# Reordering the setup of an FFT convolution: tables while h loads, x behind four tables, spectrum of h and first x stage interleaved

**Chip, cores, metric.** One core of one Trainium2 chip. The metric is device time in microseconds (us) of one execution. Besides it, this study uses landmarks: start times of named instructions in one profiled execution, counted from the start of its span.

## What is computed

```python
# x: (8, 5696, 128), h: (5696, 128)
Xf = np.fft.rfft(x, n=2*S, axis=1); Hf = np.fft.rfft(h, n=2*S, axis=0)
y  = np.fft.irfft(Xf * Hf[None], n=2*S, axis=1)[:, :S]       # causal convolution per channel
theta = y @ w_theta
out   = u + relu(u @ w_ch),  u = y + w_tok_r @ (y*cos(theta)) + w_tok_i @ (y*sin(theta))
```

The convolution is a Fourier transform of length 11392 = 178 x 64 written as matrix products: stage a (89 points by table `f`, line 190), a product with table `w` (line 208), a product with the spectrum of h, stage c (tables `r_u`, `r_v`, line 320) and stage d (table `e`). It runs once over h and then in eight groups over x. The token-mixing products after it (line 910) run from 591 us to the end, nearly three quarters of the time.

## The kernel before, as far as it matters

Every table is made on the chip: GpSimd writes an index and scales it to turns, VectorE rounds (by adding and subtracting a large constant) and subtracts, ScalarE takes sine and cosine.

```python
def turns_of(pattern, base, lanes, m, per, quarter=None):
    ...                                                     # t, k: two rotating f32 buffers, [P, 11 * NB]
    nc.gpsimd.iota(k, pattern=pattern, base=base, ...)                              # L147
    nc.gpsimd.tensor_scalar(t, k, lanes, 1.0 / per, op0=mult, op1=mult)             # L149
    nc.vector.tensor_scalar(k, t, MAGIC, None, op0=add)                             # L152
    nc.vector.scalar_tensor_tensor(t, k, MAGIC, t, op0=subtract, op1=subtract)      # L153
    return t, k
def absolute(k, r):
    nc.vector.scalar_tensor_tensor(k, r, -1.0, r, op0=mult, op1=ALU.max)            # L160

for k0 in (0, 15, 30): w_table(k0)
nc.vector.tensor_copy(h16[:NB], u_t[...])              # L224: h, one copy
x16s = {0: load_x(0)}                                  # L127: 16 loads, f32 to f16, issued by GpSimd
steps, a_h = stage_a(h16, True)                        # True: evicted by ScalarE and VectorE in turn
woven(steps, [w_table(k0) for k0 in (45, 60, 75)])
for c in range(NCK): h_chunk(c)                        # spectrum of h, 12 chunks
a0, load0, b0 = front(0)                               # stage a of x, evicted by ScalarE alone
woven(a0, [r_table(0), r_table(1), s_table] + load0)
woven(b0, [e_table(n0) for n0 in (0, 11, 22)])         # product of x's spectrum with h's
```

The order in which instructions stand on each engine is made from this by a list scheduler at build time; each engine then runs its own list strictly in order.

## Time and profile before

| | kernel before |
|---|---|
| median of 3 runs | 2176.37 us (2172.37 to 2180.45) |
| first matmul on h / first spectrum matmul / first matmul on x / first stage-c matmul | 14.85 / 30.72 / 50.45 / 86.59 us |
| busy in 0 to 87 us: VectorE, ScalarE, GpSimd | 67.8, 58.8, 41.2 us |

The prediction below shows the lines of the timeline for these landmarks and reads them. GpSimd's groups in setup are, with the number of instructions, busy us, mean ns and idle time before them (groups of 0 to 87 us):

```profile
L149 POOL TENSOR_SCALAR turn<-whole,lane 90x979 f32<-90x979 f32 x3 | 7.7, 2556 | 0.3
L149 POOL TENSOR_SCALAR turn<-whole,lane 128x960 f32<-128x960 f32 x6 | 7.1, 1188 | 0.5
L147 POOL IOTA whole<- 128x960 f32 x6 | 6.0, 1012 | 14.2 <-ACT w_t L164 14.2
L147 POOL IOTA whole<- 90x979 f32 x3 | 5.5, 1820 | 7.6 <-DVE sgn L282 4.1 <-ACT e_t L164 3.5
```

### The profile page before, as it was taken

To read this page: it belongs to the slowest core of one execution; us is meant where nothing else is said; L and a number is where in the kernel's file an instruction comes from. 1 tells how busy PE (TensorE), PEld (TensorE's weight loads), DVE (VectorE), ACT (ScalarE), POOL (GpSimd) and SP (SyncE) were. 2 spreads that over 40 slices of the span, in tenths; PEclk is the share of its full clock that TensorE was granted. 3 is DMA by queue.
4 is the path that set the end of the run, shared out by engine and by line. 5 is a ranking of instruction groups with operands and counts; after the bars stand their busy time and mean duration, and the time that the engine had idled before them with its cause. 6 is when DMAs were issued, how large, how long until landed. Compare 5 with 4: busy or idle time off the path is not lost.

```text
span 2175.5 us, 41105 instructions
## 1 busy us (share of the span) xinstructions
PE 1998.2 (92%) x15545; PEld 1125.1 (52%) x15723; DVE 1619.4 (74%) x2920; ACT 670.6 (31%) x984; POOL 857.1 (39%) x1572
## 2 busy tenths in 40 slices
PE   4788898763899999999999999899999999999998
PEld 4787888652344444444444444344444444444444
DVE  7767767767778888888877667667777777776867
ACT  5877877574132333333210000001111111111111
POOL 5301010002344645445466544354545453535350
PEclk8788889987899999999999999999999999999999
DMA  7356463579988989899999869687878787879794
GB/s 146 89 125 163 128 162 118 172 185 275 236 156 175 182 169 168 167 179 176 176 169 162 138 115 291 106 133 137 148 132 152 132 151 130 152 131 153 126 158 91
DMA packets 409382, 340.38 MB, mean 156 GB/s; under 512 B 83303, under 2 KB 363751, under 8 KB 408071
## 3 DMA queue, kind: packets, MB, share of 16 engines
q0 software_dynamic: 221312, 143.00, 48.7%
q1 hardware_dynamic: 183552, 179.93, 28.5%
q10 hardware_dynamic: 4320, 14.81, 1.8%
q8 instruction: 123, 2.02, 0.4%
q14 instruction: 75, 0.61, 0.1%
HBM read 381.83 MB, written 97.93 MB: 221 GB/s over the span
## 4 chain that ended last, share of the span: by engine, by line
PE 65%; DMA 5%; DVE 4%; issue 2%; ACT 2%; POOL 1%; SPq 1%; DVEq 0%; ACTq 0%; POOLq 0%
PE m L910 59%; DMA b<-z_hbm 3%; PE m L878 2%; DMA z_hbm<-zz 2%; DVE c L917 1%; PE v L680 1%; PE utp L673 1%; PE m L914 1%; DVE wt L591 1%; PE m L833 1%; POOL wb L582 1%; PE m L831 1%; ACT mag L404 0%; ACT red L405 0%; PE theta_ps L382 0%
## 5 line engine op out<-in xcount | busy, mean ns | idle before, releaser
L582 POOL DMA_DIRECT2D wb<-in_moe_w_tok_i_dram x720 | 387.9, 547 | 679.3 <-DVE wt L591 602.6
L591 DVE STREAM_TRANSPOSE wt<-wb 128x384 f32<-128x384 f32 (+2 forms) x720 | 360.2, 524 | 117.1 <-PE m L910 71.2
L582 POOL DMA_DIRECT2D wb<-in_moe_w_tok_r_dram x720 | 386.6, 548 | 146.2 <-DVE wt L591 107.0
L910 PE MATMUL m<-b,wt 128*128 128x512 bf16 x1803 | 425.7, 381 | 7.1 <-DVE wt L591 2.4
L910 PEld LDWEIGHTS <-wt 128*128 128x128 bf16 x1848 | 181.3, 98 | 225.0 <-issue 5.7
L917 DVE TENSOR_TENSOR c<-c,m 128x512 f32<-128x512 f32 x420 | 271.0, 671 | 0.4 <-PE m L910 0.4
L675 ACT ACTIVATE uts<-utp 128x512 bf16<-128x512 bf16 (+1 forms) x90 | 53.2, 592 | 607.3 <-PE utp L673 607.3
L320 PE MATMUL ps<-r_u,u_t 128*128 128x128 f16 x1024 | 133.0, 228 | 14.9 <-DVE u_t L304 11.7
L321 PE MATMUL ps<-r_v,v_t 128*128 128x128 f16 x1024 | 131.7, 227 | 0.0
L670 ACT ACTIVATE ub<-c 128x512 bf16<-128x512 f32 (+1 forms) x90 | 56.3, 628 | 224.9 <-DVE c L846 139.7
L127 POOL DMA_DIRECT2D x<-in_x_dram x64 | 34.2, 541 | 201.3 <-PE ps L190 189.3
L320 PEld LDWEIGHTS <-u_t 128*128 128x128 f16 x1024 | 106.0, 103 | 13.6 <-DVE u_t L304 13.5
L321 PEld LDWEIGHTS <-v_t 128*128 128x128 f16 x1024 | 104.9, 103 | 5.2 <-issue 3.7
L304 DVE TENSOR_TENSOR u_t<-xs,hs 128x1024 f16<-128x1024 f16 x96 | 69.6, 725 | 41.9 <-ACT xs L302 31.5
L302 ACT ACTIVATE xs<-ps 128x1024 f16<-128x1024 f32 x96 | 95.3, 1017 | 17.6 <-DVE v_t L304 8.7
L878 PE MATMUL m<-b,wt 128*128 128x512 bf16 x344 | 79.3, 387 | 15.3 <-ACT red L405 14.5
L190 PE MATMUL ps<-f_t,x 89*128 89x180 f16 x512 | 84.5, 310 | 8.0 <-ACT xs L302 5.9
L208 PEld LDWEIGHTS <-w_t 64*128 64x128 f16 x3240 | 65.5, 106 | 38.1 <-issue 24.7
L580 POOL COPY wb<-b 128x2 bf16<-128x2 bf16 x4 | 0.5, 179 | 213.2 <-DMA z_hbm<-zz 213.2
L190 PEld LDWEIGHTS <-x 89*128 89x128 f16 x512 | 73.8, 237 | 10.1 <-issue 9.4
L384 ACT ACTIVATE red<-theta_ps,magic 128x512 f32<-128x512 f32 (+1 forms) x46 | 31.6, 687 | 140.8 <-PE theta_ps L382 107.4
L623 ACT ACTIVATE yb<-tpz 128x512 bf16<-128x512 bf16 (+1 forms) x46 | 27.4, 597 | 153.6 <-PE tpz L621 137.4
(2713 smaller groups left out, 3824.5 us busy)
## 6 DMA issues: line engine op xcount, KB each, us to landing
wb<-in_moe_w_tok_r_dram POOLq DMA_DIRECT2D x352, 96.0 KB, 4.5
wb<-in_moe_w_tok_i_dram POOLq DMA_DIRECT2D x352, 96.0 KB, 5.0
wb<-in_moe_w_tok_r_dram POOLq DMA_DIRECT2D x352, 80.0 KB, 4.2
wb<-in_moe_w_tok_i_dram POOLq DMA_DIRECT2D x352, 80.0 KB, 3.7
hs<-hf_hbm SPq DMA_DIRECT2D x192, 128.0 KB, 3.2
cp_hbm<-c SPq DMA_DIRECT2D x88, 256.0 KB, 2.3
c<-cp_hbm SPq DMA_DIRECT2D x88, 256.0 KB, 4.0
out_dram<-c SPq DMA_DIRECT2D x88, 256.0 KB, 4.2
```

Of the source, the lines that this page charges most:

```text
L190: nc.tensor.matmul(ps[:, i // 2, (i % 2) * 2 * K1:(i % 2 + 1) * 2 * K1], lhs(q + i), f1_t[:NB], start=True, stop=True)
L208: nc.tensor.matmul(ps[:, e, j * HD:(j + 1) * HD], w_t2[rows, c0 + j, N2 * (1 - ri):N2 * (3 - ri)], a_st["a"][rows, ri * K1 + c0 + j, :], s ...
L302: nc.scalar.activation(xs[:, :, :, :ck], ps, AF.Copy)
L304: nc.vector.tensor_tensor(uv[r][:, :, :, c0:c0 + ck], xs[:, :, :, :ck], hv[:, r:r + 1, :, :ck].to_broadcast([P, 2, HD, ck]), op=mult)
L320: nc.tensor.matmul(o, u_t[:, at:at + P], r_u, start=True, stop=False)
L321: nc.tensor.matmul(o, v_t[:, at:at + P], r_v, start=False, stop=True)
L582: nc.gpsimd.dma_start(wb[32 * i:32 * i + 32, :ng, :nj * 64], bass.AP(tensor=a.tensor, offset=a.offset + row0 * S + p * H + i * QR + j0 * 6 ...
L591: nc.vector.transpose(wt.rearrange("p j t r -> p (j t r)").bitcast(F32).rearrange("p (j g t) -> p g j t", j=TJ, g=4)[:, :ng, :nj], wb[:, : ...
L670: nc.scalar.activation(ub[:m].rearrange("p b d -> p (b d)"), c[:m], AF.Copy)
L878: nc.tensor.matmul(ms[n // 2 * 2 + h], a[n][:, j, :, r], bts[jj][n % 2 * 2 + h][:, r, :], start=(n % 2 == 0 and jj == 0 and r == 0), stop= ...
L910: nc.tensor.matmul(ms[q], a[q][:, j, :, r], bts[jj][q][:, r, :], start=(jj == 0 and r == 0), stop=(jj == NJ - 1 and r == 1 and q not in left))
L917: nc.vector.tensor_tensor(c, z, ms[q], op=op)
```

## The change

The intent is to use the 12 us in which h is on its way for tables, to let the loads of x begin when four tables are made, and to run the spectrum of h and the first stage of x side by side. To make room, work per table is moved: the index is written once and reused, the rounding add goes from VectorE to GpSimd, the absolute value becomes a bit mask. Tables get smaller (9 of 640 columns and 5 of up to 623 in place of 6 of 960 and 3 of 979). Its core, cuts marked by `...`:

```diff
-        nc.gpsimd.iota(k, pattern=pattern, base=base, ...)
-        nc.gpsimd.tensor_scalar(t, k, lanes, 1.0 / per, op0=mult, op1=mult)
+        nc.gpsimd.tensor_scalar(t, index_[:m], float(base), lanes[:m], op0=add, op1=mult)
...
-        nc.vector.tensor_scalar(k, t, MAGIC, None, op0=add)
+        rounded.append(nc.gpsimd.tensor_scalar(k, t, magic[:m], 1.0, op0=add, op1=mult).ins)
         nc.vector.scalar_tensor_tensor(t, k, MAGIC, t, op0=ALU.subtract, op1=ALU.subtract)
...
-        nc.vector.scalar_tensor_tensor(k, r, -1.0, r, op0=mult, op1=ALU.max)
+        nc.vector.tensor_scalar(k.bitcast(I32), r.bitcast(I32), 0x7FFFFFFF, None, op0=ALU.bitwise_and)
...
+    r_table(0, r_u); r_table(1, r_v); s_table()                      # moved up, before the w tables
-    for k0 in (0, 15, 30): w_table(k0)
-    nc.vector.tensor_copy(h16[:NB], u_t[...])
-    x16s = {0: load_x(0)}
+    for k0 in range(0, 4 * TW, TW): last[k0] = w_table(k0)           # TW = 10
+    for d0 in range(0, HD, 16):
+        with tc.issue_after(last[TW]):                               # behind the second w table
+            nc.vector.tensor_copy(h16[:, :, :, d0:d0 + 16], u_t[...])
...
+                with tc.issue_after(rounded[-1]) if bp == 0 else ExitStack():   # each x load of pair 0
...
+    woven(steps, x_steps[:2] + w_steps[:1] + x_steps[2:4] + w_steps[1:2] + x_steps[4:])
-    for c in range(NCK): h_chunk(c)
-    woven(a0, [r_table(0), r_table(1), s_table] + load0)
-    woven(b0, [e_table(n0) ...])
+    steps, a_st = stage_a(..., g == 0)                               # first x stage on ScalarE and VectorE
+    woven((h_chunks, 0.0, 0.9), (a0, 0.1, 1.0), (load0, 0.6, 1.0), (w_steps[2:], 0.0, 0.4), (e_steps[:2], 0.5, 1.0))
+    woven(b0, (e_steps[2:], 0.0, 0.8))
```

`issue_after` fixes a place in an engine's order; it does not wait for anything.

More of the change, by code (lines that the diff above doesn't have):

```diff
@@ L13 @@
 F16 = mybir.dt.float16
+I32 = mybir.dt.int32
 add = mybir.AluOpType.add
@@ L114 @@
     uv = [t[:, :UVW].rearrange("p (e d k) -> p e d k", e=2, k=K1) for t in (u_t, v_t)]
-    h16 = s1.tile([P, 2, N2, HD], F16)
     for p0, p1 in ((0, 80), (80, NB)):
@@ L119, with part @@
                                     ap=[[N2 * D, p1 - p0], [1, N2 * D]]))
+    x16s = {}
     def load_x(bp):
-        x16 = fx.tile([P, 2, N2, D], F16, tag="x16", name="x16")
-        for e in range(2):
+        def part(e, n0):
+            if (e, n0) == (0, 0):
+                x16s[bp] = fx.tile([P, 2, N2, D], F16, tag="x16", name="x16")
             src = x[2 * bp + e]
-            for n0 in range(0, N2, 16):
-                for p0, p1 in ((0, 80), (80, NB)):
+            for p0, p1 in ((0, 80), (80, NB)):
+                with tc.issue_after(rounded[-1]) if bp == 0 else ExitStack():
                     nc.gpsimd.dma_start(
-                        x16[p0:p1, e, n0:n0 + 16, :].rearrange("p n d -> p (n d)"),
+                        x16s[bp][p0:p1, e, n0:n0 + 16, :].rearrange("p n d -> p (n d)"),
                         bass.AP(tensor=src.tensor, offset=src.offset + (p0 * N2 + n0) * D,
                                 ap=[[N2 * D, p1 - p0], [1, 16 * D]]))
-        return x16
-    lane = fc.tile([P, 2], F32)
+        return [lambda e=e, n0=n0: part(e, n0) for e in range(2) for n0 in range(0, N2, 16)]
+    lane = fc.tile([P, 5], F32)
     for p0 in (0, 64):
@@ L138, with index @@
                    allow_small_or_imprecise_dtypes=True)
-    def turns_of(pattern, base, lanes, m, per, quarter=None):
+    for c, (src, per) in enumerate(((1, N1), (0, NF), (1, NF)), 2):
+        nc.vector.tensor_scalar(lane[:, c:c + 1], lane[:, src:src + 1], 1.0 / per, None, op0=mult)
+    TW, TE = 10, 7
+    def index(pattern, pool, tag="index"):
         n = 1
@@ L144, in turns_of @@
             n *= c
-        t = s2.tile([P, 11 * NB], F32, tag="turn", name="turn")[:m, :n]
-        k = s2.tile([P, 11 * NB], F32, tag="whole", name="whole")[:m, :n]
-        nc.gpsimd.iota(k, pattern=pattern, base=base, channel_multiplier=0,
-                       allow_small_or_imprecise_dtypes=True)
-        nc.gpsimd.tensor_scalar(t, k, lanes, 1.0 / per, op0=mult, op1=mult)
+        k = pool.tile([P, n], F32, tag=tag, name="index")
+        nc.gpsimd.iota(k, pattern=pattern, base=0, channel_multiplier=0, allow_small_or_imprecise_dtypes=True)
+        return k
+    rounded = []
+    def turns_of(index_, base, lanes, m, quarter=None):
+        n = index_.shape[1]
+        room, small = (P, "_s") if n <= P else (TW * N2, "")
+        t = s2.tile([P, room], F32, tag="turn" + small, name="turn")[:m, :n]
+        k = s2.tile([P, room], F32, tag="whole" + small, name="whole")[:m, :n]
+        nc.gpsimd.tensor_scalar(t, index_[:m], float(base), lanes[:m], op0=add, op1=mult)
         if quarter is not None:
             quarter(t)
-        nc.vector.tensor_scalar(k, t, MAGIC, None, op0=add)
+        rounded.append(nc.gpsimd.tensor_scalar(k, t, magic[:m], 1.0, op0=add, op1=mult).ins)
         nc.vector.scalar_tensor_tensor(t, k, MAGIC, t, op0=ALU.subtract, op1=ALU.subtract)
@@ L166, with r_table, quarter @@
     f1_t = fc.tile([P, 2 * K1], F16)
-    t, k = turns_of([[1, K1]], 0, lane[:NB, 1:2], NB, N1)
+    t, k = turns_of(index([[1, K1]], s1, "f_index"), 0, lane[:, 2:3], NB)
     sine(f1_t[:NB, K1:], t, -1)
     cosine(f1_t[:NB, :K1], t, k)
+    r_u = fc.tile([P, P], F16)
+    r_v = fc.tile([P, P], F16)
+    sgn = fc.tile([P, N2], F32)
+    def r_table(n_, r_):
+        def quarter(t):
+            nc.vector.tensor_scalar(t, t, 1.0 / N2, None, op0=mult)
+            for q0 in range(2):
+                for q1 in range(2):
+                    a_ = t[64 * q0:64 * q0 + 64, 64 * q1:64 * q1 + 64]
+                    nc.vector.tensor_scalar(a_, a_, 0.25 * (1 + n_ + q0 - q1), None, op0=add)
+        t, k = turns_of(r_index, 0, lane[:, 0:1], P, quarter)
+        sine(k, t, 1)
+        nc.vector.tensor_scalar(r_[:, :N2 + EN], k[:, :N2 + EN], 0.125, None, op0=mult)
+        nc.vector.tensor_scalar(r_[:, N2 + EN:], k[:, N2 + EN:], -0.125, None, op0=mult)
@@ new lines, in s_table @@
+    def s_table():
+        t, k = turns_of(s_index, 0, lane[:, 1:2], P, lambda t: nc.vector.tensor_scalar(t, t, 0.5, None, op0=mult))
+        absolute(k, t)
+        nc.vector.tensor_scalar(k, k, -4.0, 1.0, op0=mult, op1=add)
+        nc.vector.memset(sgn, 1.0)
+        nc.vector.tensor_scalar(sgn[:, EN:], sgn[:, EN:], k, None, op0=mult)
+    r_index, s_index = index([[0, 2], [1, N2]], s1, "r_index"), index([[0, 1]], s1, "s_index")
+    nc.vector.tensor_scalar(s_index, s_index, 1.0, None, op0=add)
@@ L171 @@
+    r_table(0, r_u)
+    r_table(1, r_v)
+    s_table()
     w_t2 = fc.tile([P, K1, 3 * N2], F16)
+    w_index = index([[1, TW], [N1, N2]], s1)
     def w_table(k0):
-        t, k = turns_of([[1, 15], [N1, N2]], k0, lane[:, 0:1], P, NF)
+        t, k = turns_of(w_index, k0, lane[:, 3:4], P)
         t3, k3 = (z.rearrange("p (k n) -> p k n", n=N2) for z in (t, k))
-        sine(w_t2[:, k0:k0 + 15, :N2], t3, 1)
-        cosine(w_t2[:, k0:k0 + 15, N2:2 * N2], t3, k3)
-        nc.vector.tensor_scalar(w_t2[:, k0:k0 + 15, 2 * N2:], w_t2[:, k0:k0 + 15, :N2],
-                                -1.0, None, op0=mult)
@@ L181, in stage_a @@
-    def stage_a(lhs, both=False):
+        sine(w_t2[:, k0:k0 + TW, :N2], t3, 1)
+        cosine(w_t2[:, k0:k0 + TW, N2:2 * N2], t3, k3)
+        return nc.vector.tensor_scalar(w_t2[:, k0:k0 + TW, 2 * N2:], w_t2[:, k0:k0 + TW, :N2],
+                                       -1.0, None, op0=mult).ins
+    def stage_a(lhs, both=False, home=None):
         st = {}
@@ L186, in chunk @@
             if q == 0:
-                st["a"] = fa.tile([P, 2 * K1, HD], F16, tag="a", name="a_")
+                st["a"] = (home or fa).tile([P, 2 * K1, HD], F16, tag="a", name="a_")
             ps = psum()
@@ L220, in woven @@
             f()
-    for k0 in (0, 15, 30):
-        w_table(k0)
-    nc.vector.tensor_copy(h16[:NB], u_t[:NB, :N2 * D].rearrange("p (n h d) -> p h n d", h=2, d=HD))
-    x16s = {0: load_x(0)}
-    steps, a_h = stage_a(lambda q: h16[:NB].rearrange("p h n d -> p (h n) d")[:, :, q], True)
-    woven(steps, [lambda k0=k0: w_table(k0) for k0 in range(45, K1, 15)])
+    last = {}
+    for k0 in range(0, 4 * TW, TW):
+        last[k0] = w_table(k0)
+    h16 = fa.tile([P, 2 * K1, HD], F16, tag="a", name="h16").rearrange("p k d -> p (k d)")[:NB, :N2 * D].rearrange(
+        "p (h n d) -> p h n d", h=2, d=HD)
+    for d0 in range(0, HD, 16):
+        with tc.issue_after(last[TW]):
+            nc.vector.tensor_copy(h16[:, :, :, d0:d0 + 16], u_t[:NB, :N2 * D].rearrange(
+                "p (n h d) -> p h n d", h=2, d=HD)[:, :, :, d0:d0 + 16])
+    steps, a_h = stage_a(lambda q: h16.rearrange("p h n d -> p (h n) d")[:, :, q], True, s1)
+    w_steps = [lambda k0=k0: w_table(k0) for k0 in range(4 * TW, K1, TW)]
+    x_steps = load_x(0)
+    woven(steps, x_steps[:2] + w_steps[:1] + x_steps[2:4] + w_steps[1:2] + x_steps[4:])
     hst = [t[:, :6 * D * CK].rearrange("p (c h d k) -> p c h d k", c=6, h=2, k=CK) for t in (u_t, v_t)]
-    nc.gpsimd.memset(hst[(NCK - 1) // 6][:, (NCK - 1) % 6], 0.0)
+    with tc.issue_after(rounded[-1]):
+        nc.gpsimd.memset(hst[(NCK - 1) // 6][:, (NCK - 1) % 6], 0.0)
     def h_chunk(c):
@@ L247, in h_chunk @@
                 h_[64 * ri:64 * ri + 64].rearrange("p h d k -> p h (d k)"))
-    for c in range(NCK):
-        h_chunk(c)
-    nc.gpsimd.memset(u_t[:, UVW:], 0.0)
-    nc.gpsimd.memset(v_t[:, UVW:], 0.0)
-    r_u = fc.tile([P, P], F16)
-    r_v = fc.tile([P, P], F16)
-    e_t = fc.tile([P, EN, 2, NB], F16)
-    sgn = fc.tile([P, N2], F32)
-    def r_table(n_, r_):
-        def quarter(t):
-            for q0 in range(2):
-                for q1 in range(2):
-                    a_ = t[64 * q0:64 * q0 + 64, 64 * q1:64 * q1 + 64]
-                    nc.vector.tensor_scalar(a_, a_, 0.25 * (1 + n_ + q0 - q1), None, op0=add)
-        t, k = turns_of([[0, 2], [1, N2]], 0, lane[:, 0:1], P, N2, quarter)
-        sine(k, t, 1)
-        nc.vector.tensor_scalar(r_[:, :N2 + EN], k[:, :N2 + EN], 0.125, None, op0=mult)
-        nc.vector.tensor_scalar(r_[:, N2 + EN:], k[:, N2 + EN:], -0.125, None, op0=mult)
+    e_t = fc.tile([P, EN, 2, NB], F16)
     def e_table(n0):
-        t, k = turns_of([[1, 11], [N2, NB]], n0, lane[:K1, 1:2], K1, NF)
+        n = min(TE, EN - n0)
+        t, k = turns_of(e_index[:, :n * NB], n0, lane[:, 4:5], K1)
         t3, k3 = (z.rearrange("p (n m) -> p n m", m=NB) for z in (t, k))
-        sine(e_t[:K1, n0:n0 + 11, 1, :], t3, -1)
-        cosine(e_t[:K1, n0:n0 + 11, 0, :], t3, k3)
-    def s_table():
-        t, k = turns_of([[0, 1]], 1, lane[:, 1:2], P, 2)
-        absolute(k, t)
-        nc.vector.tensor_scalar(k, k, -4.0, 1.0, op0=mult, op1=add)
-        nc.vector.memset(sgn, 1.0)
-        nc.vector.tensor_scalar(sgn[:, EN:], sgn[:, EN:], k, None, op0=mult)
+        sine(e_t[:K1, n0:n0 + n, 1, :], t3, -1)
+        cosine(e_t[:K1, n0:n0 + n, 0, :], t3, k3)
     LEAD = 4
@@ L361, in front @@
         x16 = x16s[bp].rearrange("p b n d -> p (b n) d")
-        steps, a_st = stage_a(lambda q: x16[:NB, :, dh * HD + q])
+        steps, a_st = stage_a(lambda q: x16[:NB, :, dh * HD + q], g == 0)
         return (steps, *stage_b(a_st, dh))
     a0, load0, b0 = front(0)
-    woven(a0, [lambda: r_table(0, r_u), lambda: r_table(1, r_v), s_table] + load0)
-    woven(b0, [lambda n0=n0: e_table(n0) for n0 in range(0, EN, 11)])
+    with tc.issue_after(rounded[-1]):
+        nc.gpsimd.memset(u_t[:, UVW:], 0.0)
+        nc.gpsimd.memset(v_t[:, UVW:], 0.0)
+        e_index = index([[1, TE], [N2, NB]], s1, "e_index")
+    e_steps = [lambda n0=n0: e_table(n0) for n0 in range(0, EN, TE)]
+    woven(([lambda c=c: h_chunk(c) for c in range(NCK)], 0.0, 0.9), (a0, 0.1, 1.0), (load0, 0.6, 1.0), (w_steps[2:], 0.0, 0.4),
+          (e_steps[:2], 0.5, 1.0))
+    woven(b0, (e_steps[2:], 0.0, 0.8))
     setup.close()
@@ L505, in next_x @@
             def next_x(bp=bp):
-                x16s[bp + 1] = load_x(bp + 1)
+                for part in load_x(bp + 1):
+                    part()
             a_ = a_ + [next_x]
```

## The prediction

> **What bounds the kernel now.** I read the page first, to see how much of the span the change can touch at all, then the timeline of the first 90 us, then the waits of that stretch, then the busy times by stage.
>
> The page, parts 2 and 4:
>
> ```profile
> PE   4788898763899999999999999899999999999998
> ...
> PE 65%; DMA 5%; DVE 4%; issue 2%; ACT 2%; POOL 1%; SPq 1%; DVEq 0%; ACTq 0%; POOLq 0%
> PE m L910 59%; DMA b<-z_hbm 3%; PE m L878 2%; DMA z_hbm<-zz 2%; DVE c L917 1%; PE v L680 1%; PE utp L673 1%; PE m L914 1%; DVE wt L591 1%; PE m L833 1%; POOL wb L582 1%; PE m L831 1%; ACT mag L404 0%; ACT red L405 0%; PE theta_ps L382 0%
> ```
>
> The end is set by TensorE: 59% of the chain is the token-mixing product (line 910), which the change does not touch. One slice is 54.4 us, and the first has TensorE at 4 tenths. Everything the change edits runs before the first matmul of stage c (line 320). The two programs' instruction orders were compared with line numbers and buffer numbers removed: beyond that point they are the same but for a few neighbours near the first stage c (and a swap of two neighbours late on TensorE). So the change is worth what it moves that one matmul, which the timeline puts at 86.59 us. Its landmarks:
>
> ```profile
> 12.51 2.29 DVE L224 COPY h<-u_t 89x8192 f16<-89x8192 f16 x1 [6.69 <-DMA u_t<-in_h_dram]
> ...
> 14.85 5.64 PE L190 MATMUL ps<-f_t,h 89*128 89x180 f16 x36 [14.85 <-DVE h L224]
> ...
> 20.11 0.99 POOL L147 IOTA whole<- 128x960 f32 x1 [9.47 <-ACT w_t L164]
> ...
> 30.72 4.42 PE L208 MATMUL ps<-a__163,w_t 64*128 64x64 f16 x159 [3.69 <-DVE a__163 L195]
> ...
> 50.45 0.92 PE L190 MATMUL ps<-f_t,x 89*128 89x180 f16 x4
> ...
> 63.61 3.35 PE L208 MATMUL ps<-a__707,w_t 64*128 64x64 f16 x128 [1.88 <-ACT a__707 L197]
> ...
> 86.59 0.29 PE L320 MATMUL ps<-r_u,u_t 128*128 128x128 f16 x1 [3.05 <-DVE u_t L304]
> ```
>
> Setup therefore has five legs: wait for h (to 14.85), first stage of h (to 30.7), spectrum of h (to 50.4), first stage of x (to 63.6), product with the spectrum (to 86.6). VectorE ends the last one. Busy time in three stretches (0 to 38, 38 to 63.6, 63.6 to 86.6):
>
> ```profile
> core 0: us, PE busy (x) PEld busy (x) DVE busy (x) ACT busy (x) POOL busy (x), PEclk, DMA share, GB/s
> 0.00:38.00 38.00, 15.38 (x244) 14.16 (x244) 24.16 (x35) 16.85 (x21) 23.78 (x42) 1.00 0.71 130
> 38.00:63.60 25.60, 15.82 (x244) 14.74 (x245) 21.21 (x37) 21.47 (x27) 12.50 (x12) 0.52 0.57 144
> 63.60:86.60 23.00, 12.38 (x373) 10.93 (x373) 21.98 (x32) 20.12 (x21) 4.95 (x2) 0.57 0.36 107
> ```
>
> From 38 us on VectorE is busy 43.2 of 48.6 us and ScalarE 41.6: these two share the bound. VectorE's large hole is early, 13.8 us before 38, nearly all of it while h loads. What filled its time, from the costliest groups of 0 to 87 us:
>
> ```profile
> L195 DVE CAST a__163<-ps 128x720 f16<-128x720 f32 x8 | 7.1, 898 | 0.0
> L160 DVE SCALAR_TENSOR_TENSOR whole<-turn 128x960 f32<-128x960 f32 x6 | 7.0, 1161 | 0.0
> L153 DVE SCALAR_TENSOR_TENSOR turn<-whole,turn 128x960 f32<-128x960 f32 x6 | 6.9, 1149 | 0.1
> ...
> L152 DVE TENSOR_SCALAR whole<-turn 128x960 f32<-128x960 f32 x6 | 3.9, 658 | 0.0
> ```
>
> **What the Trainium skill says.** "VectorE: DVE Perf Modes", section Mode 2×_2P: a one-source fp32 operation in SBUF uses both read ports and makes two results a cycle, an operation with two tensors cannot. The trace agrees: 658 ns against 1161 ns for the same 128x960. The new absolute value is a one-source operation, so I count it at the first rate; no record here shows a bitwise operation. "GPSIMD Engine Reference", section Specifications: GpSimd's SBUF interfaces are shared with VectorE, with contention when VectorE is in a two-port mode or has two SBUF inputs. The trace agrees: the 90x979 scaling on GpSimd took 1.40 us at 61.4 and 3.85 us at 67.5, beside products on VectorE. "DMA: Bandwidth & Descriptors", section SWDGE vs HWDGE vs iDMA: a cast during a transfer is to be had on the GpSimd path only. So the x loads (f32 to f16) must stand in GpSimd's program, and do: 12 of the 16 stood behind the iota that waited 9.47 us. "TensorE: Matmul & The Clock Gate", section What's actually happening: low activity halves the clock. Here it is 0.52 from 38 to 63.6 us; TensorE is busy 15.8 of 25.6 us there, so I give it no term.
>
> **The change part by part.** Sizes between measured ones are interpolated from 128 and 960 columns (tensor_scalar 0.23 and 0.66 us, two-input form 0.29 and 1.15, sine 0.40 and 1.10, GpSimd scaling 0.37 and 1.06): at 640 columns 0.49, 0.82, 0.83, 0.80 us.
>
> 1. Tables. The rounding add leaves VectorE (6 x 0.66 + 3 x 0.66 and small ones, about 6.4 us by their uncontended times) for GpSimd, which loses its 6 + 3 large iotas (11.5 us). Absolute values fall from 6 x 1.16 + 3 x 1.17 = 10.5 to 14 x 0.48 = 6.7 us. Smaller tables (9 of 640 and 5 of up to 623 in place of 6 and 3) add the fixed part of the other operations, some 2 us.
> 2. The first x stage is split between ScalarE and VectorE: 8 casts of 0.90 = 7.2 us come to VectorE, 8 of 0.83 leave ScalarE. Sum for VectorE: -6.4 - 3.8 + 2 + 7.2 = about -1. Its total of 67.4 us hardly falls; the gain has to come from filling the hole.
> 3. Start. Tables f, r_u, r_v, s and the first w run while h loads. h had landed at 12.5 with x traffic beside it; now some 12. The copy of 2.29 us becomes four of about 0.6, the first ending near 13.6: the first h matmul is about 1 us earlier.
> 4. First stage of h. VectorE between first copy and end: three copies 1.8, eight casts 7.2, w work 3.5 = 12.5 us, so it ends near 26 and the spectrum starts near 26.5, not 30.7: -4.
> 5. x. GpSimd's list up to the fourth table sums to about 10 us after 4.7, so the first x load issues near 15, not 5. The 16 loads are 8 x 320 + 8 x 36 KB = 2.9 MB; from 22 to 30 us x moved at 123 to 148 GB/s, mean 134: 21.8 us. Last landing about 37.5. In the kernel before, 0.7 MB had landed by 15 and the rest ran from 22 to about 38, yet its first x matmul was at 50.45, so x was not waited for. In the new TensorE order the first x matmuls stand after only two of twelve spectrum chunks: near 28.5 us the in-order engines reach x and stand until about 37.5. I expect a new wait of 7 to 9 us here; it eats step 4.
> 6. From there VectorE's order holds: 8 casts 7.2, 4.25 spectrum evictions 5.3, 8 absolute values 3.8, 3 negations 0.9, 7 subtractions 5.5, one scaling 0.45 = 23.1; then 22 products starting 0.605 apart and two short ones, 14.0. Sum 37.1, from 37.5 + 0.8 for the first four matmuls. Stalls: as before, 48.6 - 43.2 = 5.4 us. 38.3 + 37.1 + 5.4 = 80.8 us for the first stage-c matmul. ScalarE from the same point: 6.4 + 5.1 + 10.2 + 13.9 = 35.6, below VectorE.
>
> Gain: 86.6 - 80.8 = 5.8 us; 2176.4 - 5.8 = 2170.6. The change was presumably kept by its author for a gain, so I shade to 2170.
>
> **Rivals.** (a) x arrives early or its wait costs nothing, and the interleaved phase starts at 28.5: then VectorE ends at 28.5 + 0.8 + 37.1 + 5.4 = 72 us, a gain of 15 and 2162. Against it: the same 2.9 MB at the measured rate, issued later. (b) GpSimd becomes the bound: 8 tables x 2 operations x 0.8 us = 13 us after the last x issue near 29, but 2.4 to 3.9 us each where contended as at 57 and 67 us, which would pass 60 us and hold the last e tables, now all ahead of the first product in VectorE's order. That costs 3 to 8 us: 2173 to 2178. For it: doubled GpSimd arithmetic, more two-port work. Against: before, two thirds of such scalings were near 1.1 us. (c) The gain is swallowed later: nothing after is on a fixed clock, and the chain is TensorE work in order, so I take it as passed on whole.
>
> **Range and chances.** Setup is 87 us; 2% is 43.5, half of it. Neither rival comes near. The range takes rival (a) with a little more at its low end, 2161, and rival (b) at its high end, 2177; the three runs of before alone span 8 us. Faster by over 2%: 0.01; within: 0.98; slower: 0.01.
>
> **What would show it.** First h matmul near 13.6; first spectrum matmul near 26.5; a wait of TensorE for an x load of 7 us or more, ending at 36 to 39; first stage-c matmul near 81; absolute value of 640 columns near 0.5 us; the rest of the timeline shifted by one amount. Wrong if x comes before 32, if GpSimd holds VectorE before the products, or if the shift at stage c is not found at the end.

## The result

| | kernel before | changed kernel |
|---|---|---|
| median | 2177.46 us (4 runs) | 2178.61 us (4 runs) |
| range | 2172.37 to 2180.45 | 2174.57 to 2179.82 |
| ratio | | 1.0004, 95% interval 0.9981 to 1.0028 |
| first stage-c matmul | 86.59 | 85.89 us |

Nothing was gained. A ratio here and below is the mean time of one kernel's fast runs over that of the other's of the same rounds, so not quite the ratio of the medians. The forecast time, 2170, lay outside what was measured.

The landmarks in the timeline of the changed kernel (start and duration in us, engine, line, operation; in brackets how long the engine had stood and what ended that):

```profile
18.41 0.68 DVE L274 COPY h<-u_t 89x2048 f16<-89x2048 f16 x1
...
19.14 3.24 PE L235 MATMUL ps<-f_t,h 89*128 89x180 f16 x20 [19.14 <-DVE h L274]
...
32.23 1.89 PE L253 MATMUL ps<-a__205,w_t 64*128 64x64 f16 x64 [2.15 <-DVE a__205 L240]
...
38.59 1.47 PE L235 MATMUL ps<-f_t,x 89*128 89x180 f16 x8 [4.47 <-DMA x<-in_x_dram]
...
64.33 4.45 PE L253 MATMUL ps<-a__425,w_t 64*128 64x64 f16 x160 [1.33 <-DVE a__425 L240]
...
85.89 0.29 PE L347 MATMUL ps<-r_u,u_t 128*128 128x128 f16 x1 [2.44 <-DVE u_t L331]
```

Three readings. The copy of h has no wait in its brackets: h had landed, and the copy merely stood behind table work, so h starts 4.3 us later than before (19.14 against 14.85), not 1 us earlier. TensorE does stand for x, as predicted, but begins the spectrum only at 32.23 and so waits 4.5 us and not 9. And from x on the setup takes 47.3 us in place of the 43.3 predicted (37.5 to 80.8).

The busy times of the two stretches, before and after the first matmul on x:

```profile
core 0: us, PE busy (x) PEld busy (x) DVE busy (x) ACT busy (x) POOL busy (x), PEclk, DMA share, GB/s
0.00:38.59 38.59, 12.05 (x129) 11.24 (x129) 27.27 (x63) 19.15 (x26) 31.92 (x58) 1.00 0.64 120
38.59:85.90 47.31, 33.98 (x733) 29.01 (x733) 41.42 (x57) 38.75 (x44) 16.19 (x14) 0.85 0.52 139
```

In the first row the busiest engine is GpSimd: 31.9 of 38.6 us. In the kernel before it was busy 23.8 us of the first 38. GpSimd's groups of the changed kernel in 0 to 87 us:

```profile
L163 POOL TENSOR_SCALAR turn<-index,lane 128x640 f32<-128x640 f32 x9 | 9.7, 1081 | 6.8 <-DVE whole L174 6.4
L130 POOL DMA_DIRECT2D x<-in_x_dram x16 | 9.0, 569 | 0.5 <-DMA x<-in_x_dram 0.5
L166 POOL TENSOR_SCALAR whole<-turn,magic 128x640 f32<-128x640 f32 x9 | 9.0, 1000 | 0.2
L166 POOL TENSOR_SCALAR whole<-turn,magic 90x623 f32<-90x623 f32 x4 | 5.2, 1302 | 0.7 <-ACT e_t L178 0.4
L163 POOL TENSOR_SCALAR turn<-index,lane 90x623 f32<-90x623 f32 x4 | 4.3, 1086 | 9.1 <-ACT a__425 L242 6.8 <-DVE whole L174 2.3
```

The rounding add (line 166) takes 17.2 us here: 9.0 + 5.2 in these two rows, and 1.6 + 0.7 + 0.7 in the smaller groups. On VectorE it had been estimated at 6.4 us, and measured at 3.9 + 3.8 for the large tables. The iotas that were saved took 11.5. The sum of GpSimd in setup rose from 41.2 to 48.1 us. Its order shows what that does to x (GpSimd's timeline):

```profile
12.88 2.36 POOL L166 TENSOR_SCALAR whole<-turn,magic 128x128 f32<-128x128 f32 x3 [0.25 <-DVE turn L195]
15.77 1.31 POOL L163 TENSOR_SCALAR turn<-index,lane 128x640 f32<-128x640 f32 x1 [0.53 <-DVE whole L174]
17.17 0.89 POOL L166 TENSOR_SCALAR whole<-turn,magic 128x640 f32<-128x640 f32 x1
18.01 2.76 POOL L130 DMA_DIRECT2D x<-in_x_dram  x4
20.86 2.86 POOL L163 TENSOR_SCALAR turn<-index,lane 128x640 f32<-128x640 f32 x2
23.71 0.83 POOL L166 TENSOR_SCALAR whole<-turn,magic 128x640 f32<-128x640 f32 x1
24.49 2.11 POOL L130 DMA_DIRECT2D x<-in_x_dram  x4
26.64 0.81 POOL L166 TENSOR_SCALAR whole<-turn,magic 128x640 f32<-128x640 f32 x1
27.41 3.13 POOL L130 DMA_DIRECT2D x<-in_x_dram  x6
31.00 1.03 POOL L130 DMA_DIRECT2D x<-in_x_dram  x2 [0.47 <-DMA x<-in_x_dram]
```

GpSimd has hardly a gap from 13 to 32 us, and the x loads stand in between its table work: the first at 18.0, the last at 31.5 us. This list placed the x loads. From 23 to 27 us, after GpSimd had been at tables from 20.9 to 24.5, the transfers ran at 52 GB/s; from 27 to 32 us, with loads queued, they ran at 202 GB/s with the DMA engines busy throughout, so at the end of the list the transfers bind as well.

### The profile page after: what moved, and what is told of

The parts are those of the page before. It is cut to its first block, busy times and chain, and to the rows that moved or that the text cites. A ratio compares the mean times of both kernels' runs of the same rounds, so it can differ in the third digit from the quotient of the medians.

```text
span 2177.3 us, 41171 instructions
## 1 busy us (share of the span) xinstructions
PE 2001.1 (92%) x15545; PEld 1123.9 (52%) x15723; DVE 1621.2 (74%) x2938; ACT 669.3 (31%) x986; POOL 864.4 (40%) x1587
## 4 chain that ended last, share of the span: by engine, by line
PE 75%; DVE 8%; DMA 7%; ACT 4%; issue 3%; POOL 1%; SPq 1%; ACTq 0%; DVEq 0%; POOLq 0%
PE m L944 57%; PE m L912 3%; PE ps L347 3%; PE ps L348 3%; PE ps L235 2%; DMA b<-z_hbm 2%; DMA z_hbm<-zz 2%; DVE c L951 2%; PE ps L370 1%; DMA hs<-hf_hbm 1%; PE ps L253 1%; ACT xs L329 1%; PE v L714 1%; DVE wt L625 1%; PE utp L707 1%
## 5 line engine op out<-in xcount | busy, mean ns | idle before, releaser
L130 POOL DMA_DIRECT2D x<-in_x_dram x64 | 33.8, 535 | 204.2 <-PE ps L235 191.9
L329 ACT ACTIVATE xs<-ps 128x1024 f16<-128x1024 f32 x96 | 95.0, 1015 | 18.8 <-DVE v_t L331 9.8
L657 ACT ACTIVATE yb<-tpz 128x512 bf16<-128x512 bf16 (+1 forms) x46 | 27.5, 597 | 154.8 <-PE tpz L655 120.8
L417 ACT ACTIVATE red<-theta_ps,magic 128x512 f32<-128x512 f32 (+1 forms) x46 | 31.6, 687 | 136.1 <-PE theta_ps L415 107.3
```

The costliest lines, as they stand in the source:

```text
L329: nc.scalar.activation(xs[:, :, :, :ck], ps, AF.Copy)
```

## The experiments

The whole time tells apart 0.2% at best, about 4 us, so the first stage-c matmul is the main measure, and the whole time is given where it was taken in rounds. All runs but one were correct. Landmarks in us, busy times of VectorE (V), ScalarE (A) and GpSimd (G) before and after the first matmul on x:

| run | first h | spectrum | last x issue | first x | stage c | V, A, G to x | V, A, G from x | from stage c to the end |
|---|---|---|---|---|---|---|---|---|
| kernel before | 14.9 | 30.7 | 29.1 | 50.5 | 86.6 | 35.6, 25.6, 28.1 | 31.7, 32.9, 13.1 | 2088.9 |
| before_again | 15.0 | 30.8 | 29.3 | 50.5 | 86.6 | 35.6, 25.6, 27.8 | 31.7, 32.8, 13.3 | 2088.9 |
| changed kernel | 19.1 | 32.2 | 31.5 | 38.6 | 85.9 | 27.3, 19.2, 31.9 | 41.4, 38.8, 16.2 | 2091.4 |
| after_again | 19.2 | 32.2 | 31.2 | 38.7 | 84.8 | 27.0, 19.2, 32.3 | 41.6, 38.9, 16.2 | 2094.3 |
| h_early | 13.2 | 30.5 | 33.0 | 41.3 | 86.7 | 29.9, 19.3, 32.8 | 39.9, 38.7, 14.6 | 2091.3 |
| x_free | 16.0 | 32.6 | 32.5 | 40.7 | 86.3 | 29.4, 19.1, 35.7 | 40.1, 38.7, 14.8 | 2092.7 |
| hx | 13.6 | 32.0 | 32.5 | 39.5 | 85.0 | 30.3, 18.8, 33.0 | 40.0, 38.5, 14.8 | 2088.4 |
| pool_tiny | 16.2 | 27.2 | 26.7 | 33.8 | 76.4 | 28.9, 19.7, 25.6 | 38.0, 37.3, 6.5 | 2095.1 |
| round_dve | 19.2 | 32.3 | 27.2 | 34.4 | 81.7 | 29.2, 17.3, 22.8 | 45.3, 40.5, 9.4 | 2093.4 |
| a0_act | 19.1 | 32.2 | 31.4 | 38.6 | 86.9 | 27.2, 19.1, 32.1 | 35.5, 42.7, 14.2 | 2090.0 |
| seq | 19.1 | 32.2 | 31.5 | 50.0 | 83.0 | 36.9, 27.9, 39.4 | 29.0, 29.1, 10.5 | 2089.1 |
| seq_round | 19.2 | 32.2 | 27.0 | 48.1 | 82.2 | 42.7, 27.5, 26.6 | 31.7, 29.4, 5.6 | 2089.6 |
| seq_round_h | 13.3 | 31.6 | 32.3 | 49.2 | 83.3 | 41.7, 27.6, 26.7 | 31.8, 29.4, 5.6 | 2092.1 |
| seq_act_h | 13.7 | 29.1 | 32.4 | 50.3 | 83.2 | 35.3, 37.8, 26.5 | 29.0, 31.0, 2.8 | 2090.7 |
| act_only | 16.3 | 29.6 | 28.4 | 35.4 | 80.0 | 26.6, 25.6, 23.8 | 39.0, 43.1, 10.3 | 2091.5 |
| act_only_5 | 16.3 | 29.6 | 29.2 | 35.7 | 80.3 | 27.5, 25.6, 24.0 | 38.9, 43.1, 10.1 | 2091.6 |
| abs_old | 22.7 | 37.5 | 32.3 | 39.7 | 89.2 | 30.3, 18.0, 31.3 | 46.4, 41.1, 18.0 | 2090.6 |

One reservation holds for all of them. The list scheduler makes the orders anew for every edit, so no edited run changes one thing alone: of these runs only after_again has the changed kernel's order on VectorE. The first copy of h, for example, is the 40th of VectorE's instructions in the changed kernel, the 38th in act_only and the 44th in abs_old. No run holds the order fixed.

**Does a landmark repeat?** after_again is the changed kernel unaltered (no edit).

> The changed kernel unaltered, to learn how far its landmarks repeat. Every theory expects the first matmul on h at 19 us, the first on x at 38 to 39 us and the first stage-c matmul at 85 to 87 us (85.9 before). If the last one moves by 2 us or more, differences of that size in the other runs mean nothing.

It came at 84.8 us: 1.1 us from the first look. The later before_again, the kernel before unaltered:

> The kernel before, unaltered. Every theory that compares landmarks needs the first spectrum matmul at 30 to 31.5 us, the first on x at 49.5 to 51.5 and stage c at 85.5 to 87.5. If stage c is below 84 or above 89, one look at each kernel is not enough to compare them.

It came at 86.6, as the first look. So differences of 2 us at stage c can be read, and the setup of the changed kernel ends 0.7 to 1.8 us before the old one. From stage c to the end, looks at one kernel differ by up to 3 us. The clock that TensorE was granted plays no part that shows: from 38 to 63.6 us it was 0.52 in one look at the kernel before and 1.00 in the other, with TensorE busy 15.8 us in both and the same landmarks to 0.1 us. So the low clock there, which the prediction puts down to low activity, did not come with the same activity a second time.

**Theories A and B.** A: the arrival of x ends the first half and VectorE's list the second. B: the gain was lost with the late copy of h. h_early:

```diff
+    r_table(0, r_u); last[0] = w_table(0)
-        with tc.issue_after(last[TW]):        # the copies
+        with tc.issue_after(last[0]):
+    with tc.issue_after(copied):              # VectorE's part of r_v, s, w(10), w(20), w(30) behind the copies
+        r_table(1, r_v); s_table(); ...
```

> The four copies of h are queued behind table w(0) alone, and the tables r_v, s, w(10), w(20), w(30) behind the copies. Theory A (what ends setup is the arrival of x and the VectorE work queued behind it): the first matmul on h falls from 19.1 to 13.5 to 14.5 us, the first on x stays at 38 to 39 us, and the first stage-c matmul stays within 1.5 us of 85.9. Theory B (the gain was lost because h was copied 6 us after it had landed): the first stage-c matmul falls by 4 to 6 us, to about 81.

The copy came at 12.4 and the first matmul on h at 13.2, and stage c at 86.7: the 4 to 6 us of B do not appear. A holds for stage c but not for the way: x came 2.7 us later, and the spectrum began only 1.7 us earlier. TensorE's timeline shows where the 6 us went:

```profile
13.17 3.84 PE L233 MATMUL ps<-f_t,h 89*128 89x180 f16 x24 [13.17 <-DVE h L271]
22.07 1.46 PE L233 MATMUL ps<-f_t,h 89*128 89x180 f16 x8 [5.06 <-DVE a__205 L238]
```

After six chunks it stood 5.06 us for an eviction by VectorE, which stood in VectorE's order behind tables: VectorE worked on these from 15.4 to 21.1 us, with one gap of 0.3 us. Since x came later too, this run does not give the effect of an earlier h alone. Time over 4 runs: ratio 1.0011 (0.9994 to 1.0028). x_free:

```diff
-                with tc.issue_after(rounded[-1]) if bp == 0 else ExitStack():
+                with ExitStack():
```

> The x loads are no longer queued behind the fourth table; nothing else changes. First x issue about 11 us in place of 18.0, so x is complete near 32 in place of 38.4. Theory A: the first matmul on x falls to 33 to 34 us, and the first stage-c matmul by 3 to 5 us, to 81 to 83. Theory B: h is still copied at 18.4 or later, and the first stage-c matmul stays within 1.5 us of 85.9, because tables are held up by the issues on GpSimd.

The first x load was issued at 10.9 us in place of 18.0, and the last still at 32.5; x came 2 us later than in the changed kernel. A fails as well in what it said of this run: starting x early does not bring x early, since the loads are spread among GpSimd's table operations and move those back. Ratio 1.0008 (0.9985 to 1.0032). hx has both edits:

> Both edits together. Theory A alone: as x_free, 81 to 83 us for the first stage-c matmul. Theory B alone: as h_early, about 81. If each held the other (h first, then x), the two together give more than either: 76 to 79 us, and the whole kernel 2168 to 2172.

Stage c at 85.0, ratio 0.9999 (0.9976 to 1.0022): no gain either. With the changed kernel's, four orders of the same GpSimd work all end its last x issue at 31 to 33 us, with GpSimd busy for 79 to 88% of the time to x. That led to theory C.

**Theory C: GpSimd holds the setup.** pool_tiny takes GpSimd's large operations down to 16 columns and leaves every other engine its instructions (though not their order). Its output is wrong, which doesn't matter for the time.

```diff
-        nc.gpsimd.tensor_scalar(t, index_[:m], float(base), lanes[:m], ...)
+        nc.gpsimd.tensor_scalar(t[:, :16], index_[:m, :16], float(base), lanes[:m], ...)   # large tables only
-        rounded.append(nc.gpsimd.tensor_scalar(k, t, magic[:m], 1.0, ...).ins)
+        rounded.append(nc.gpsimd.tensor_scalar(k[:, :16], t[:, :16], magic[:m], 1.0, ...).ins)
```

> Wrong result on purpose: GpSimd's two operations per large table write 16 columns in place of 445 to 640 (the table buffers are filled once at the start, and the sines get a scale near zero so that their arguments stay legal); VectorE, ScalarE, TensorE and the transfers keep all their instructions. Theory C (GpSimd holds setup: its list delays the x issues, and its operations stretch VectorE's through the shared SBUF interface): last x issue falls from 31.5 to about 27, first matmul on x to 34 to 36 us, VectorE's busy time from there to stage c from 41.5 to 37 to 38.5 us, the first stage-c matmul to 77 to 81. Rival A (the work of VectorE and ScalarE sets it whatever GpSimd does): VectorE stays at 41 us busy or more and stage c at 84 to 86.

All four numbers moved as C said, two of them a little further: last x issue 26.7 (expected about 27), first x 33.75 (34 to 36), VectorE 37.96 us busy from there (37 to 38.5), stage c 76.4 (77 to 81), which is 9.5 us earlier than in the first look at the changed kernel. The stretch from x on:

```profile
33.75:76.40 42.65, 33.27 (x733) 28.82 (x733) 37.96 (x54) 37.30 (x43) 6.49 (x12) 0.87 0.57 152
```

Against the changed kernel's row above, 4.8 us of the 9.5 come before x and 4.7 after it. Two parts of C are not equally large. VectorE's busy time up to stage c is 66.8 in place of 68.7 us, with four buffer fills of 0.6 us more, so its other instructions took some 4.3 us less. VectorE's idle time fell from 17.2 to 9.6 us (85.9 - 68.7 and 76.4 - 66.8). Its waits that GpSimd ended up to stage c add up to 10.9 us in the changed kernel, 2.3 in pool_tiny and 7.7 in the kernel before; the wait for the rounded turns is the largest in the changed kernel (us in total, times, longest; then the same in pool_tiny):

```profile
DVE turn L167 <- POOL whole L166: 6.1, 7, 2.3
```

```profile
DVE turn L176 <- POOL whole L175: 1.1, 4, 0.4
```

So most of the gain is waiting for GpSimd's list that is gone.

round_dve undoes one line of the change, the place of the rounding add:

```diff
-        rounded.append(nc.gpsimd.tensor_scalar(k, t, magic[:m], 1.0, op0=add, op1=mult).ins)
+        nc.vector.tensor_scalar(k, t, MAGIC, None, op0=add)      # `rounded` takes the scaling operation instead
```

> The rounding add goes back from GpSimd to VectorE, all else as in the changed kernel. Theory C: GpSimd has 14 operations of about 1 us less, the last x issue comes near 26 and the first matmul on x at 33 to 36 us; VectorE gets 14 operations of 0.49 us more, 8 of them after that point, partly paid by shorter ones; first stage-c matmul 81 to 84. Rival A: VectorE only gains work, stage c at 87 to 90.

```profile
34.41 1.48 PE L235 MATMUL ps<-f_t,x 89*128 89x180 f16 x8 [0.17 <-issue]
...
81.74 0.29 PE L347 MATMUL ps<-r_u,u_t 128*128 128x128 f16 x1 [2.35 <-DVE u_t L331]
```

Last x issue 27.2 (expected near 26), first x 34.4 and no longer waited for, stage c 81.7: as C expected, although VectorE is busy 74.5 us in all in place of 68.7. The whole gain lies before x; from x to stage c it takes 47.3 us, as in the changed kernel. Rival A, which expected 87 to 90, fails. Ratio to the kernel before 0.9986 (0.9962 to 1.0009).

act_only gives the same line to ScalarE:

```diff
+        nc.scalar.activation(k, t, AF.Identity, bias=magic[:m])
```

> The changed kernel with the rounding add on ScalarE and the interleaving kept. Theory C: the first matmul on x again falls to 33.5 to 36 us, as with the rounding on VectorE, since GpSimd's list is the same; stage c at 80 to 84. If the place of the rounding mattered only through VectorE's load, the first matmul on x would stay at 38 to 39.

First x 35.4, stage c 80.0, the best of all correct versions. ScalarE paid 10.8 us (57.9 to 68.7 up to stage c). The sum of GpSimd up to there fell from 48.1 to 34.0. With more rounds:

> The changed kernel with the rounding add on ScalarE, again and timed. Stage c within 1.5 us of the 80.0 of the first look. If the 5 us at stage c are passed on to the end: ratio to the kernel before 0.996 to 0.9985. If something later swallows them: 0.9985 to 1.001.

Stage c again at 80.3, and 2174.00 us (5 runs) against 2177.41 for the kernel before (9 runs): ratio 0.9979, interval 0.9965 to 0.9992. The ratio lies where it was expected if the gain is passed on, though the interval reaches into the other range. This is the one version that is faster than the kernel before beyond the noise, by 0.2%; the changed kernel, at 1.0004, was timed in another round. Its timeline against that of the changed kernel:

```profile
35.74 1.47 PE L235 MATMUL ps<-f_t,x 89*128 89x180 f16 x8 [4.29 <-DMA x<-in_x_dram]
...
80.28 0.29 PE L347 MATMUL ps<-r_u,u_t 128*128 128x128 f16 x1 [2.00 <-DVE u_t L331]
```

**The other parts.** a0_act evicts the first x stage by ScalarE alone, as before:

```diff
-        steps, a_st = stage_a(lambda q: x16[:NB, :, dh * HD + q], g == 0)
+        steps, a_st = stage_a(lambda q: x16[:NB, :, dh * HD + q])
```

> The first x stage is evicted by ScalarE alone again: 8 casts of 0.90 us leave VectorE, 8 of 0.83 come to ScalarE, whose busy time after x goes from 38.8 to 45.5 of some 46 us. If VectorE alone ends setup, stage c falls by 3 us or more, to 81 to 83. If the two are balanced there, ScalarE takes its place and stage c comes at 86 to 90.

VectorE lost 6 us and ScalarE got 4; stage c at 86.9, 1 to 2 us later. That is in the second expectation's range, but hardly more than two looks at one kernel differ by: the first expectation, VectorE alone, fails, and the split of that stage was worth 2 us at most. abs_old puts the old absolute value back:

```diff
-        nc.vector.tensor_scalar(k.bitcast(I32), r.bitcast(I32), 0x7FFFFFFF, None, op0=ALU.bitwise_and)
+        nc.vector.scalar_tensor_tensor(k, r, -1.0, r, op0=mult, op1=ALU.max)
```

> The changed kernel with the absolute value in its old two-input form: 14 operations of 0.82 in place of 0.49 us on VectorE, 4.6 us in all, 2.5 of them after the first matmul on x. If VectorE's sum sets the end after x: stage c at 87 to 89.5. If GpSimd's list does, which the two-input form contends with as well: 85 to 87.

Stage c at 89.2, some 3 to 4 us later. This is not the bit mask alone: in the order made for this run the copies of h stand behind more table work, so the first matmul on h is 3.6 us later already (22.7 against 19.1). seq undoes the interleaving alone:

```diff
-    woven((h_chunks, 0.0, 0.9), (a0, 0.1, 1.0), (load0, 0.6, 1.0), (w_steps[2:], 0.0, 0.4), (e_steps[:2], 0.5, 1.0))
+    woven(h_chunks, (w_steps[2:], 0.0, 0.4))
+    woven(a0, load0, e_steps[:2])
```

> The interleaving alone is undone: twelve spectrum chunks of h first, then the first stage of x. If the interleaving is worth something, stage c comes at 89 to 92 in place of 85 to 86 us; if what ends setup is the sum of VectorE's and ScalarE's work, it stays within 2 us, at 84 to 88, with the first matmul on x near 50 and no wait for x.

Stage c at 83.0, earlier than with the interleaving by 2 to 3 us; neither expectation was for that (the second allowed 84 to 88). With the spectrum first, there is no stretch in which TensorE, VectorE and ScalarE stand behind x in order. The interleaving cost time here, as long as x comes at 38.6; with x at 34.4 it costs nothing that shows (81.7 in round_dve, 82.2 in seq_round below).

**Combining.** seq_round has both edits, seq_round_h adds h_early, seq_act_h has the rounding on ScalarE in place of VectorE.

> The two edits that brought stage c forward, together: rounding on VectorE and no interleaving. If the gains add (2.4 and 3.7 us off the mean 85.4 of the two looks at the changed kernel) stage c comes at 78 to 80 us. If both only remove the same wait for x, they do not add: 81 to 83.

> As seq_round, with the copies of h queued behind table w(0) alone and the other early tables behind them. Without interleaving the first matmul on x stands after the spectrum, so no wait for x is left to swallow an earlier h: if GpSimd was what hid the late copy, the first spectrum matmul falls from 32.3 to 28 to 29.5 us and stage c to 76 to 79. If VectorE's sum sets the end, it stays where seq_round is, within 1 us. Whole kernel 2167 to 2172.

> As seq_round_h, with the rounding add on ScalarE (Identity with a bias): some 11 us of work on ScalarE, 7 us less on VectorE, and GpSimd free of it as well. If VectorE's sum sets the end, stage c comes 2 to 5 us before seq_round_h, at 73 to 77. If ScalarE becomes the bound, at or behind seq_round_h, 78 to 82.

Stage c at 82.2, 83.3 and 83.2; ratios 0.9985 (0.9963 to 1.0007), 0.9984 (0.9967 to 1.0002) and 0.9983 (0.9964 to 1.0002). The gains do not add, as seq_round's second expectation had it: seq and round_dve each leave TensorE without the 4.5 us wait for x, and there is no second such wait to remove. The earlier h bought nothing once more, not even without the wait for x: in seq_round_h h comes 5.9 us earlier than in seq_round, the spectrum 0.6 us, stage c 1.1 us later. seq_act_h missed both of its ranges. In seq_act_h neither VectorE (64.4 us busy up to stage c), ScalarE (68.8) nor GpSimd (29.3) is full; what limits it was not followed further.

## Why the prediction was wrong, step by step

- **Only setup moves; under 2%.** Right.
- **Step 1, tables.** This is the step that failed. It booked the 6.4 us that leave VectorE, and set the rounding that GpSimd gains against the iotas that it loses (11.5 us) without costing it. At the rates in the profile of before (1.19 us for 960 columns on GpSimd, 2.56 us for 979 where contended, against 0.66 on VectorE) eighteen further GpSimd operations could have been costed. They took 17.2 us and GpSimd's sum to stage c rose by 6.9; the first x load was issued at 18.0 us and not near 15; and VectorE stood 10.9 us for GpSimd, 7.7 before. With the rounding off GpSimd stage c comes some 4 us (round_dve) and 5 us (act_only, twice) earlier. The bit mask was sized right: 0.48 us uncontended for 640 columns.
- **Step 2, eviction by two engines.** VectorE's sum was to fall by 1 us and rose by 1 (67.4 to 68.7).
- **Steps 3 and 4, h.** First h at 13.6 and spectrum at 26.5 were predicted, 19.1 and 32.2 measured. The order of VectorE, which could be read before, has the copies of h behind the second and third w tables, and the prediction gave those tables no time. h_early and seq_round_h, with h 6 us earlier, have stage c no earlier; but x came later in both, so what this miss cost by itself is not isolated.
- **Step 5, x.** 37.5 predicted, 38.6 measured: near by luck, as the terms missed in opposite directions. The first load came 3 us late, and the 134 GB/s that were to hold throughout were 52 GB/s from 23 to 27 us, after GpSimd had been at tables from 20.9 to 24.5, and 202 GB/s from 27 to 32. The step let all 16 loads follow the fourth table; twelve stand behind the fifth or sixth. In round_dve, with the same transfers, x is there at 34.4. The wait predicted for TensorE (7 to 9 us) was there, 4.5 us long.
- **Step 6, from x to stage c.** 43.3 us predicted (37.5 to 80.8), 47.3 measured: VectorE was busy 41.4 us in place of 37.1, and 5.9 idle in place of 5.4 and 0.8 for the first matmuls. VectorE has one subtraction more than the sum had (8 and not 7, some 0.8 us); the rest of the 4.3 us is instructions that took longer than when uncontended: subtractions of 640 columns 1.12 us on average for 0.82, absolute values 0.80 for 0.48, negations 0.68 for 0.31. pool_tiny has 42.65 us and 37.96 busy, but two subtractions and one absolute value fewer after x, so its nearness to the predicted sum is in part chance.
- **Rival (b), GpSimd as the bound,** was named with 3 to 8 us and put aside because two thirds of such operations had been near 1.1 us. That is a mean per operation. The list was summed up to the fourth table (10 us) and after the last x load (13 us), but not in between, where the x loads stand among the tables. GpSimd as the bound is what happened, though not only as named: of VectorE's 10.9 us of waits for it, 4.8 come after x, where the rival had them. That stage c comes at 80.0 to 81.7 with the rounding elsewhere, near the predicted 80.8, does not confirm the sum: VectorE was busy 65.7 to 74.5 us in those runs.
- **Rival (c), passed on whole.** Not settled. From stage c to the end both looks at the kernel before took 2088.9 us, the fifteen looks at the others 2088.4 to 2095.1, on average 2091.4. For act_only the medians show 3.4 us of the 6.3 gained at stage c. The two kernels run the same instructions there but for the exchange of a few neighbours, so I can't name what takes the 2.5 us, nor exclude that two looks at the kernel before happened to be low. Eleven runs of the kernel before in one round span 13 us (2171.50 to 2184.70), while its stage c repeated to 0.02 us.

## What to carry to other kernels

When work is moved off a full engine, cost it on the engine that receives it, instruction by instruction, and add up that engine's whole list to the point that matters; an engine that also issues transfers passes its delay on to what those transfers feed (here the last x load 4.3 us earlier in round_dve, x 4.2 us earlier). A change of order may not help while one list holds the rest: here four orders ended within 2 us of each other at stage c, and moving one line gained 4 to 5 us. And interleaving on in-order engines is a bet on the arrival of the later input.

## What the Trainium skill lacked or had wrong

- "GPSIMD Engine Reference", section 4.1 Engine selection: it calls one-input elementwise work on GpSimd roughly line-rate, without a fixed part and without company. In these runs an f32 scaling took 0.37 us for 128 columns and 0.80 for 640 at the least, so 0.84 ns a column and some 0.26 us fixed, and 1.08 us on average for 640 in setup; the same rounding add of 640 columns took 0.50 us on average on VectorE and 0.86 on ScalarE.
- "GPSIMD Engine Reference", section Specifications: it names the contention with VectorE without a size for elementwise work. In the changed kernel GpSimd's scaling of 640 columns took 0.80 to 1.62 us, and VectorE's bit mask of 640 columns 0.47 to 1.10.
- "VectorE: DVE Perf Modes", section Mode 2×_2P: it does not name bitwise operations. An AND of int32, 128x640, took 0.48 us, the rate of the add of f32, and not the 0.81 us of the two-input form.
- "DMA: Bandwidth & Descriptors", section Bandwidth: its table of loads issued from GpSimd has 341 GB/s for 1 MB and no row for loads that cast. Here the f32 to f16 loads of x landed at 123 to 148 GB/s from 22 to 30 us in the kernel before and at 202 from 27 to 32 us in the changed kernel, counted at the destination.
- No page spells out what order on GpSimd means for a load that must be issued there: it also waits for GpSimd's elementwise work. That cost 4 us here (first matmul on x 38.6 against 34.4 us).
